# A three-part network on one core: its first stage written in the order of a list scheduler, the token-mixing remainder spread over three channel steps, and the causal mask moved to VectorE

## The chip, the cores and the metric

The kernel runs on one core of one Trainium2 chip, in one launch. The metric is device time in microseconds (us), median of several runs. Engines are named as in the profile: PE is TensorE (matmuls and transposes), PEld its weight loads, DVE is VectorE, ACT is ScalarE, POOL is GpSimd, SP is SyncE, which issues all transfers here.

## The reference, cut to what matters

Three layers follow each other (4 batches, 576 positions, width 512):

```
# 1: attention, 8 heads of width 64; 4x pooled attention plus a band of |i - j| < 4
out_d = sm_attn(mean4(q), mean4(k), mean4(v));  out_up = repeat(out_d, 4)
scores = where(|i - j| < 4, 0.125 * q k^T, -1e9);  out_local = softmax(scores) v
x = out_up + out_local
# 2: mixing over tokens (576 -> 256 -> 576), then over channels (512 -> 1536 -> 512)
u = x + (relu(x^T w_tok1) w_tok2)^T
x = u + relu(u w_ch1) w_ch2
# 3: four experts, each a causal attention head; the two best experts of a position count
scores = where(causal, -1e9, 0.125 * q k^T);  out += mask * weight * (softmax(scores) v wo)
```

The four mixing weights come in as float64 and are turned into a high and a low float32 part on the chip; a product of two such pairs is three matmuls.

## The kernel before, in words

**First stage.** The attention has 16 units (a batch `b` and a pair of heads `p`). A unit loads q, k and v (`load_qk`, `load_v`), computes local and pooled scores (`scores`: PE tiles `sl` and `sd`, row maxima on DVE in `nmx` and `nd`, exponentials on ACT, normalisation on POOL), transposes the weights (`turns`: `pdt`, `tl`) and multiplies with v (`values`: `pod`, `ol`; DVE adds into `u`). Two units make a half (8 halves), which goes through token mixing: transposes (`tx`, `tok_turn`), the first product (`h`, `tok_first`) and the second (`pu`, `tok_second`, added to `u` by DVE). Besides, 7 pieces of token weights and 6 pieces of channel weights are converted from float64 in this stage: per piece two ACT instructions (`t`, `g`), three of DVE (`a`, `f`, `f` again: L200 to L202), one add on POOL (L206), then the high part on ACT and the low part on DVE (L143, L153).

The loop at L508 calls these as whole steps, in the order given by `ORDER`, with priorities from `PRI`; the tile framework's own scheduler then lays out each engine's queue. All token weights are converted ahead of the loop (`START`, `tok_weights`), one channel piece per unit from the fourth on (`CONV0`).

**Channel stage.** `ch_step` (L569): 4 groups of hidden channels by 5 blocks of columns, 1440 matmuls of some 460 columns into tiles `c`. Token mixing of the last half is called ahead of the first steps (`TAIL`), which the scheduler fills in between.

**Third stage.** `score` (L712) computes one tile of scores of one expert: two matmuls `s<-K,Q`, and a third, `s<-caus,identb`, which adds -1e9 above the diagonal (80 tiles, one mask matmul each). DVE takes the row maximum (`nm`, L734), ACT the exponential from PSUM with the sum (L737), DVE the normalisation (L738 to L740). Projections, transposes (`pt`), products with v (`o`) and the output (`wo`) fill PE around them.

Every PE instruction but a transpose has line L108 in the profile, so tiles tell them apart.

Of the kernel before, what the change touches and what calls it, by code (L numbers as in the profile page):

```python
# [45 lines left out]
PRI = {'K': 100, 'a': 30, 'W': -60, 'S': 30}  # L46
VEC = {'k': 3, 'v': 1}
KTWICE = True
ZENG = ['any', 'any']
PRE = False  # L50
QPOOL = 'vector'
KPOOL = 'gpsimd'
ABANKS, CBANKS = (4, 2), (6, 1)
START = 'q0 q1 q2 v0 w v1 v2'
XLO = 'gpsimd'
CONV0 = 3
UB = 5
TAIL = [0, 3, 4, 3]
ULO = 'vector'
LA = 2  # L60
DELAY = 0
ORDER = 'VKTCFWS'
VB = 3
KB = 3


@with_exitstack
def body(ctx, tc, qT, kT, vw, vp, wt1, wt2, wc1, wc2, wq, wk, wvg, wo, out):
# [24 lines left out]
    def spare(kind, i=0):  # L93

        return nc.vector if i < VEC.get(kind, 0) else nc.gpsimd

# [20 lines left out]
    caus = cst.tile([128, TQ], BF16, name="caus")  # L117
# [7 lines left out]
    for hf in range(2):  # L125
# [6 lines left out]
    nc.gpsimd.affine_select(out=caus, in_=caus, compare_op=OP.is_ge, fill=-1.0e9, base=0,  # L132
                            pattern=[[-1, TQ]], channel_multiplier=1)
# [7 lines left out]

    def split(hi, lo, src, relu=False, scale=None):
        nc.scalar.activation(hi, src, AF.Relu if relu else AF.Copy, **({"scale": scale} if scale else {}))  # L143
        lowpart(lo, src, hi, relu, scale)
# [18 lines left out]
    def flat(t, shape):  # L163
        return t.rearrange("p c n -> p (c n)") if len(shape) == 3 else t

# [8 lines left out]
    def load_f32(dram, shape, name, dst=None):  # L174

        P0, n = shape[0], 1
        for d in shape[1:]:
            n *= d
        if dram.dtype == F32:
            if dst is None:  # L180
                dst = pv.tile(shape, F32, tag="w64t", bufs=2, name=name + "_t")
            nc.sync.dma_start(dst, dram)
            return dst
        raw = pv.tile([P0, n, 2], I32, tag="raw64", bufs=2, name=name + "_raw")
        d32 = dram.bitcast(I32)
        if len(shape) == 3:
            nc.sync.dma_start(raw.rearrange("p (c n) t -> p c (n t)", c=shape[1]), d32)
        else:
            nc.sync.dma_start(raw.rearrange("p n t -> p (n t)"), d32)
        h = raw[:, :, 1]  # L190
        a = pv.tile([P0, n], I32, tag="w64a", bufs=2, name=name + "_a")
        f = pv.tile([P0, n], I32, tag="w64f", bufs=2, name=name + "_f")
        g = pv.tile([P0, n], F32, tag="w64g", bufs=2, name=name + "_g")
        t = pv.tile([P0, n], F32, tag="w64t", bufs=2, name=name + "_t")

        nc.scalar.activation(t.bitcast(I32), raw.bitcast(U32)[:, :, 0], AF.Copy, scale=2.0 ** -29)  # L196

        nc.scalar.activation(g, h.bitcast(F32), AF.Abs)

        nc.vector.tensor_scalar(a, h, 3, 0x3FFFFFF8, op0=OP.logical_shift_left, op1=OP.bitwise_and)  # L200
        nc.vector.scalar_tensor_tensor(f, h, -0x40000000, a, op0=OP.bitwise_and, op1=OP.bitwise_or)
        nc.vector.scalar_tensor_tensor(f.bitcast(F32), g, 2.0 ** -15, f.bitcast(F32), op0=OP.is_ge, op1=OP.mult)  # L202
        if dst is None:
            dst = t.rearrange("p (c n) -> p c n", c=shape[1]) if len(shape) == 3 else t

        nc.gpsimd.tensor_tensor(flat(dst, shape).bitcast(I32), f, t.bitcast(I32), op=OP.add)  # L206
        return dst
# [20 lines left out]
    def tok_split(dram, shape, name):  # L228
        hi = pt.tile(shape, F32R, name=name + "_hi")
        lo = pt.tile(shape, F32R, name=name + "_lo")  # L230
        split(flat(hi, shape), flat(lo, shape), flat(load_f32(dram, shape, name), shape))
        return hi, lo

    tok = {}

    def tok_weights():
        w1 = []
        for t in range(0, 4, 2):
            hi, lo = tok_split(wt1[128 * t:128 * t + 256].rearrange("(t p) j -> p t j", t=2), [128, 2, DT], f"wt1_{t}")
            w1 += [(hi[:, i], lo[:, i]) for i in range(2)]  # L240
        wr = [pt.tile([128, DT], F32R, name=f"wt1_r{x}") for x in "hl"]
        nc.gpsimd.memset(wr[1][REM:].bitcast(F32), 0.0)
        src = load_f32(wt1[512:S], [REM, DT], "wt1_4")
        split(wr[0][:REM], wr[1][:REM], src)
        nc.scalar.activation(wr[0][REM:], src, AF.Copy)
        tok["w1"] = w1, wr
        w2 = [[tok_split(wt2[m * 128:(m + 1) * 128, s * HS:(s + 1) * HS], [128, HS], f"wt2_{m}{s}")
               for s in range(2)] for m in range(2)]
        tok["w2"] = w2


# [8 lines left out]
    Vl, Vd = {}, {}  # L260

    def load_v(b, p):
        i = b * NP + p
        if i < VB:
            zero(VZ, i, getattr(nc, ZENG[1]))
            nc.gpsimd.memset(VX[i], 0.0)
        Vl[b, p] = VZ[(b * NP + p) % VB]
        for h in range(2):
            nc.sync.dma_start(Vl[b, p][64 * h:64 * h + 64, h], vw[b, p, 64 * h:64 * h + 64])
        raw = pa.tile([112, 3, 4, D], F32, tag="vp", bufs=1, name=f"vp{b}{p}")  # L270
        nc.sync.dma_start(raw, vp[b, p])
        vd = pa.tile([112, 2, D], F32, tag="vd", bufs=3, name=f"vd{b}{p}")
        vx = VX[(b * NP + p) % VB]
        i = b * NP + p
        spare("v", i).tensor_tensor(raw[:, :, 0:2], raw[:, :, 0:2], raw[:, :, 2:4], op=OP.add)
        spare("w", i).tensor_tensor(vd, raw[:, 0::2, 0], raw[:, 0::2, 1], op=OP.add)
        nc.gpsimd.tensor_tensor(vx[:64, 0], raw[:64, 1, 0], raw[:64, 1, 1], op=OP.add)
        nc.gpsimd.tensor_tensor(vx[64:112, 1], raw[64:, 1, 0], raw[64:, 1, 1], op=OP.add)
        Vd[b, p] = (vd, vx)

    QK = {}

    def load_qk(b, p):
        q = pa.tile([128, S], F32, tag="qT", bufs=3, name=f"qT{b}_{p}")
        nc.sync.dma_start(q, qT[b, p])
        i = b * NP + p
        if i < KB:
            zero(KZ, i, getattr(nc, ZENG[0]))
        kz = KZ[i % KB]
        for h in range(2):  # L290
            nc.sync.dma_start(kz[64 * h:64 * h + 64, h], kT[b, p, 64 * h:64 * h + 64])
        k = None
        if KTWICE:
            k = pa.tile([128, S], F32, tag="kT", bufs=3, name=f"kT{b}_{p}")
            nc.sync.dma_start(k, kT[b, p])
        QK[b, p] = (q, k, kz)

    SC = {}

    def scores(b, p):  # L300
        qt, kt, kz = QK.pop((b, p))

        def pool4(d, x, eng):
            x4 = x.rearrange("p (g r) -> p g r", r=4)
            if eng == "vector":
                nc.vector.tensor_reduce(d, x4, axis=AX.X, op=OP.add)
            else:
                a = pa.tile([128, SD, 2], F32, tag="pool2", bufs=2, name="pool2")[:d.shape[0]]
                nc.gpsimd.tensor_tensor(a, x4[:, :, 0:2], x4[:, :, 2:4], op=OP.add)
                nc.gpsimd.tensor_tensor(d, a[:, :, 0], a[:, :, 1], op=OP.add)  # L310

        qd = pa.tile([128, SD], F32, tag="qd", bufs=3, name="qd")
        kd = pa.tile([128, SD], F32, tag="kd", bufs=3, name="kd")
        pool4(qd, qt, QPOOL)
        if KTWICE:
            pool4(kd, kt, KPOOL)
        else:
            for h in range(2):
                o = slice(64 * h, 64 * h + 64)
                nc.vector.tensor_reduce(kd[o], kz[o, h].rearrange("p (g r) -> p g r", r=4), axis=AX.X, op=OP.add)  # L320

        ps = b2("sl")
        for h in range(2):
            mm(ps[:, h, :NW * 32].rearrange("p (t k) -> p t k", k=WIN), identb,
                             band[:, None, :].to_broadcast([128, NW // 2, WIN]), start=True, stop=False)
        for w in range(NW):
            o, g = 64 * (w % 2), 2 * (w // 2)
            cols = slice(KS[w], KS[w] + WIN)

            for h0, h1 in [(0, 2)] if g != NT - 1 else [(0, 1), (1, 2)]:  # L330
                bk, c0 = (g + h0) // NT, (g + h0) % NT * WIN
                mm(ps[o:o + 64, bk, c0:c0 + (h1 - h0) * WIN].rearrange("p (h k) -> p h k", k=WIN),
                                 qt[:, cols], kz[:, h0:h1, cols], start=False, stop=(g + h1) % NT == 0)
        sv = ps[:, :, :NW * 32].rearrange("p b (t k) -> p b t k", k=WIN)
        nmx = pa.tile([128, 2, NT], F32, tag="nmx", bufs=3, name="nmx")
        nc.vector.tensor_reduce(nmx, sv, axis=AX.X, op=OP.max, negate=True)
        nc.vector.tensor_scalar_mul(nmx, nmx, 0.125)  # L337
# [129 lines left out]
    for what in START.split():  # L467
        if what == "w":
            with ahead("I"):
                tok_weights()  # L470
# [464 lines left out]
```

## Time and profile before

| | |
|---|---|
| median of 3 runs | 740.4 us (740.32 to 742.41) |
| the profiled execution, its own time | 743.14 us |
| its span, first to last instruction | 741.4 us |
| PE busy in the span | 680.7 us, 92% |
| PEld | 593.2 us, 80% |
| DVE | 478.1 us, 64% |
| ACT | 387.5 us, 52% |
| POOL | 162.5 us, 22% |
| mean granted TensorE clock (1 is 2.4 GHz, 0.5 is 1.2 GHz) | 0.961 |

Busy time counts any instruction that has begun and not ended, also while it is held up inside; a matmul's end is modelled, and matmuls overlap, so a price of PE work is read from one start to the next. Shares over the whole span mix three stages: the first channel matmul starts at 219.0 us and the last ends at 529.1 us. "Idle before" is the time an engine waited ahead of an instruction, with what ended the wait.

### The profile page before, as it was taken

The numbers are of one execution on the slowest core, as the hardware profiler recorded it, in microseconds if no ns is written. First come the engines' busy times: TensorE is split into PE (matmuls) and PEld (weight loads), VectorE is DVE, ScalarE is ACT, GpSimd is POOL, SyncE is SP. The second block draws the span as 40 slices with busy tenths as digits, with TensorE's granted clock in tenths as the row PEclk, the third lists the DMA queues.
The fourth block names the chain that finished last, engine by engine and source line by source line (L and its number), as shares of the span: only waits on it lengthen the run. The fifth ranks groups of instructions, "written<-read, shape, count | busy, mean of one in ns | idle before, by whom it ended". The sixth has DMA issues, their size and how long they took to land.

```text
span 741.4 us, 13335 instructions
## 1 busy us (share of the span) xinstructions
PE 680.7 (92%) x4892; PEld 593.2 (80%) x4892; DVE 478.1 (64%) x1076; ACT 387.5 (52%) x1236; POOL 162.5 (22%) x197
## 2 busy tenths in 40 slices
PE   3468889889999999999999999999998999999987
PEld 2346777667888998888888898888886988889875
DVE  4899986556554796764665464443268777777873
ACT  6577667556643564433532232222157776686674
POOL 4777864443210222100110000000312030010000
PEclk8767899999999999999999999999999999999999
DMA  9978564423000231200101010000020022021102
GB/s 249 268 228 229 166 187 121 126 75 101 20 1 1 67 104 61 78 33 1 58 15 42 1 31 26 2 1 0 1 65 17 17 61 62 21 85 33 33 29 100
DMA packets 31761, 52.26 MB, mean 70 GB/s; under 512 B 3728, under 2 KB 16528, under 8 KB 31696
## 3 DMA queue, kind: packets, MB, share of 16 engines
q1 hardware_dynamic: 31696, 51.40, 23.8%
q8 instruction: 39, 0.64, 0.4%
q14 instruction: 26, 0.21, 0.1%
HBM read 41.95 MB, written 4.72 MB: 63 GB/s over the span
## 4 chain that ended last, share of the span: by engine, by line
PE 81%; DVE 8%; ACT 4%; DMA 3%; POOL 1%; issue 1%; SPq 0%; ACTq 0%; POOLq 0%; DVEq 0%
PE c L108 41%; PE proj L108 7%; PE vp L108 4%; PE s L108 4%; PE o L108 4%; PE h L108 3%; PE wo L108 3%; PE ol L108 3%; PE pu L108 3%; PE sl L108 3%; PE pt L111 3%; DMA qT<-in_qT_dram 2%; PE pod L108 2%; PE tx L111 1%; ACT P L343 1%
## 5 line engine op out<-in xcount | busy, mean ns | idle before, releaser
L108 PE MATMUL c<-hh,wcl 128*128 128x460 f32 (+1 forms) x240 | 89.2, 372 | 0.0
L108 PE MATMUL c<-uh,wcl 128*128 128x460 f32 (+1 forms) x240 | 89.2, 372 | 0.0
L108 PE MATMUL c<-ul,wch 128*128 128x460 f32 (+1 forms) x240 | 89.1, 371 | 0.0
L108 PE MATMUL c<-hl,wch 128*128 128x460 f32 (+1 forms) x240 | 89.1, 371 | 0.0
L108 PE MATMUL c<-hh,wch 128*128 128x460 f32 (+1 forms) x240 | 89.1, 371 | 0.0
L108 PE MATMUL c<-uh,wch 128*128 128x460 f32 (+1 forms) x240 | 89.1, 372 | 0.0
L143 ACT ACTIVATE hh<-c 128x460 fp32r<-128x460 f32 (+1 forms) x60 | 33.1, 551 | 98.9 <-PE c L108 98.4
L149 DVE SCALAR_TENSOR_TENSOR hl<-c,hh 128x460 fp32r<-128x460 f32 (+1 forms) x60 | 38.1, 634 | 53.4 <-ACT hh L143 53.3
L206 POOL TENSOR_TENSOR wc_t<-wc_f,wc_t 128x512 int32<-128x512 int32 x24 | 33.5, 1400 | 159.4 <-ACT wc_t L196 142.1
L541 ACT ACTIVATE uh<-u 128x460 fp32r<-128x460 f32 (+1 forms) x80 | 46.2, 586 | 34.6 <-PE c L108 23.5
L343 ACT ACTIVATE P<-sl,nmx 128x64 f32<-128x64 f32 x160 | 48.1, 332 | 26.4 <-DVE nmx L337 19.9
L542 DVE TENSOR_TENSOR ul<-u,uh 128x460 fp32r<-128x460 f32 (+1 forms) x80 | 49.8, 634 | 11.5 <-ACT uh L541 11.5
L737 ACT ACTIVATE Pc<-s,nm 112x576 f32<-112x576 f32 (+4 forms) x80 | 44.4, 560 | 16.0 <-DVE nm L734 15.8
L108 PEld LDWEIGHTS c<-hl,wch 128*128 128x128 f32 x240 | 45.2, 188 | 5.2
L108 PEld LDWEIGHTS c<-uh,wcl 128*128 128x128 f32 x240 | 45.2, 188 | 5.3
L108 PEld LDWEIGHTS c<-ul,wch 128*128 128x128 f32 x240 | 45.2, 188 | 5.1
L108 PEld LDWEIGHTS c<-uh,wch 128*128 128x128 f32 x240 | 45.1, 188 | 5.0
L108 PEld LDWEIGHTS c<-hh,wch 128*128 128x128 f32 x240 | 45.1, 188 | 5.1
L108 PEld LDWEIGHTS c<-hh,wcl 128*128 128x128 f32 x240 | 45.1, 188 | 5.0
L734 DVE TENSOR_REDUCE nm<-s 112x1 f32<-112x576 f32 (+4 forms) x80 | 40.5, 514 | 11.7 <-PE s L108 10.2
L108 PE MATMUL s<-K,Q 128*112 128x288 f32 (+3 forms) x192 | 42.7, 320 | 3.5 <-DVE Q L151 1.8
L740 DVE TENSOR_SCALAR Pc<-Pc,su,gw 112x576 f32<-112x576 f32 (+4 forms) x80 | 38.3, 480 | 2.3
(180 smaller groups left out, 1767.3 us busy)
## 6 DMA issues: line engine op xcount, KB each, us to landing
wc_raw<-in_wc_dram SPq DMA_DIRECT2D x24, 512.0 KB, 3.7
vp<-in_vp_dram SPq DMA_DIRECT2D x16, 336.0 KB, 3.4
vz<-in_vw_dram SPq DMA_DIRECT2D x32, 160.0 KB, 3.6
qT<-in_qT_dram SPq DMA_DIRECT2D x16, 288.0 KB, 4.3
kz<-in_kT_dram SPq DMA_DIRECT2D x32, 144.0 KB, 4.6
kT<-in_kT_dram SPq DMA_DIRECT2D x16, 288.0 KB, 4.5
K<-K SPq DMA_DIRECT2D x64, 72.0 KB, 2.0
out_dram<-y SPq DMA_DIRECT2D x18, 256.0 KB, 2.0
```

The costliest lines, as they stand in the source:

```text
L108: behind(nc.tensor.matmul(*a, **kw))
L111: behind(nc.tensor.transpose(*a))
L143: nc.scalar.activation(hi, src, AF.Relu if relu else AF.Copy, **({"scale": scale} if scale else {}))
L149: nc.vector.scalar_tensor_tensor(lo, src, 0.0, h, op0=OP.max, op1=OP.subtract)
L206: nc.gpsimd.tensor_tensor(flat(dst, shape).bitcast(I32), f, t.bitcast(I32), op=OP.add)
L343: nc.scalar.activation(P[:, t, h], sv[:, bk, i], AF.Exp, bias=nmx[:, bk, i:i + 1], scale=0.125, accum_out=sm[:, t, h:h + 1])
L541: nc.scalar.activation(hi, u, AF.Copy)
L542: getattr(nc, ULO).tensor_tensor(lo, u, hi.bitcast(F32), op=OP.subtract)
L734: nc.vector.tensor_reduce(nm[:nq], sv, axis=AX.X if t < 4 else AX.XY, op=OP.max, negate=True)
L737: nc.scalar.activation(pv_, sv, AF.Exp, bias=nm[:nq], accum_out=su[:nq])
L740: nc.vector.tensor_scalar(P[:nq, :n], P[:nq, :n], su[:nq], ST[b]["W"][:nq, t, 2 * p + e:2 * p + e + 1], op0=OP.mult, op1=OP.mult)
```

## The change

The first stage is now made of 25 kinds of single steps (`unit`, `half`, `convert_f64`; for example `sl`, `mx`, `ex`, `rs`, `P` in place of the first part of `scores`). `first_stage` writes down for each step its engine, a duration (`COST`), what it waits for, what buffers it holds, and a rank; `arrange` runs a list scheduler over them while the kernel is built, and the steps are issued in that order under a manual schedule, so each engine's queue has it. Conversions get ranks of their own (`CONV`): a token piece every 1.1 units from the start, a channel piece every 1.8 units from the fourth.

```diff
+CONV = (2.8, 11.1, 37.6, 17.7)
+SLACK = 0.17
...
+        op("mx", i, "DVE", [("sl", i, None)])
+        op("ex", i, "ACT", [("mx", i, None)], [("P", [("tl", i, 1)])])
...
+        t, r, n = min(can)
+        eng = ops[n][0]
+        t, r, n = min((c for c in can if ops[c[2]][0] == eng and c[0] <= t + SLACK), key=lambda c: (c[1], c[0]))
...
+    steps = arrange(first_stage())
+    cut = max(k for k, n in enumerate(steps) if n[0] in U_[0] or n[0] not in H_[0]) + 1
+    with tc.manual_schedule():
+        for n in steps[:cut]:
+            do(*n)
...
-    tail = [lambda i=i, w=w: tok_step(i, w) for i in range(n, n + 2 + DELAY) for w in "KFW"]
+    tail = steps[cut:]
+    share = -(-len(tail) // TAIL)
     for i in range(len(seq) + 1):
...
+        if i < TAIL:
+            with ahead("T"):
+                for n in tail[i * share:(i + 1) * share]:
+                    do(*n)
```

What is left of token mixing after the last attention step and conversion (`tail`) is split evenly over the first three channel steps. Three smaller edits in the first stage: the pooled product with `vx` is two matmuls of 64 output rows in place of one of 128; the first unit's v sum goes from DVE to POOL (`VEC` is gone); and the zeroing of buffers, which was shared out over DVE and ACT, is on DVE (k) and POOL (v).

```diff
-        mm(po[:, :SD], vx.rearrange("p h d -> p (h d)"), PdT[:, 1], start=False, stop=True)
+            for h in range(2):
+                mm(po[64 * h:64 * h + 64, :SD], vx[:, h], PdT[:, 1], start=False, stop=True)
```

In the third stage the mask matmul is gone. One DVE instruction adds a float32 mask to the scores, writes them negated to SBUF and takes their minimum; ACT reads them there. The mask constant grows from 116 columns of bf16 to 580 of float32.

```diff
-    caus = cst.tile([128, TQ], BF16, name="caus")
+    caus = cst.tile([128, NT * TQ], F32, name="caus")
...
-            if m0 < m1:
-                mm(ps[:nq, m0 - a0:m1 - a0], identb[:nq, :nq], caus[:nq, m0 - d0:m1 - d0],
-                                 start=False, stop=True)
...
-        nc.vector.tensor_reduce(nm[:nq], sv, axis=AX.X if t < 4 else AX.XY, op=OP.max, negate=True)
...
-        nc.scalar.activation(pv_, sv, AF.Exp, bias=nm[:nq], accum_out=su[:nq])
+        mask = caus[:nq, 4 * TQ - d0:4 * TQ + nq]
...
+        nc.vector.tensor_tensor_reduce(pv_, sv, mask, -1.0, 3.0e38, OP.add, OP.min, nm[:nq])
+        nc.scalar.activation(P[:nq, :n], P[:nq, :n], AF.Exp, bias=nm[:nq], scale=-1.0, accum_out=su[:nq])
```

How the queues moved, at three places. DVE in the first stage, before, where the third unit's maximum is taken; `wt_01`, `wt_10`, `wt_11` and `wc_0` are weight pieces, all else is of units:

```order
L337 TENSOR_SCALAR nmx<-nmx 128x10
L200 TENSOR_SCALAR wt_01_a<-wt_01_raw 128x288
L201 SCALAR_TENSOR_TENSOR wt_01_f<-wt_01_raw,wt_01_a 128x288
L202 SCALAR_TENSOR_TENSOR wt_01_f<-wt_01_g,wt_01_f 128x288
L357 TENSOR_REDUCE nd<-sd 72x4
L306 TENSOR_REDUCE qd<-qT_1_682 128x144
L200 TENSOR_SCALAR wt_10_a<-wt_10_raw 128x288
L358 TENSOR_SCALAR nd<-nd 72x4
L414 TENSOR_TENSOR u<-ol,OdT 128x232
L201 SCALAR_TENSOR_TENSOR wt_10_f<-wt_10_raw,wt_10_a 128x288
```

The same queue now, from the maximum of the fourth unit; the next conversion, that of `wt_01`, comes 31 rows behind the first of these:

```order
L462 TENSOR_REDUCE nmx<-sl 128x10
L463 TENSOR_SCALAR nmx<-nmx 128x10
L476 TENSOR_SCALAR rs<-sm 128x10
L477 RECIPROCAL rs<-rs 128x10
L565 TENSOR_TENSOR u<-ol,OdT 128x232
L565 TENSOR_TENSOR u<-ol,OdT 128x344
L492 TENSOR_REDUCE nd<-sd 72x4
L493 TENSOR_SCALAR nd<-nd 72x4
L428 TENSOR_REDUCE qd<-qT_1_518 128x144
```

Conversions stood between the steps of a unit and now stand units apart; all 7 token pieces had come ahead of the fifth unit's maximum and now reach to the eighth's.

PE at the end of the first stage, now, where the transposes of the seventh half (`tx`) and its first product (`h`) meet the first channel tile (`c`):

```order
L222 MATMUL pu<-wt_11h,h1l 128x288
L225 MATMUL tx_2880<-ident,u 128x128 x4
L225 MATMUL tx_2886<-ident,u 128x128 x4
L225 MATMUL tx_2894<-ident,u 64x128 x2
L222 MATMUL h_2905<-xh,wt_0h 128x256
L222 MATMUL h_2905<-xl,wt_0h 128x256
L222 MATMUL h_2905<-xh,wt_0l 128x256
L222 MATMUL h_2905<-xh,wt_0h 128x256
L222 MATMUL h_2905<-xl,wt_0h 128x256
L222 MATMUL h_2905<-xh,wt_0l 128x256
L222 MATMUL h_2905<-xh,wt_2h 128x256
L222 MATMUL c_2936<-uh,wch_114 128x462
```

Before, all of the seventh half stood ahead of the first `c`; now most of its first product, its second product and the whole eighth half follow behind it.

DVE in the third stage, now (a tile of 232, one of 576 columns); the fused instruction is followed by a second one that writes the minimum:

```order
L875 ISA Pc,nm<-s,caus 116x232
L875 ISA nm 116x1
L875 ISA Pc,nm<-s,caus 112x576
L875 ISA nm 112x1
L878 RECIPROCAL su<-su 116x1
```

Before, one TENSOR_REDUCE (L734) stood in the place of each such pair; there are 80 pairs.

## Rows read from the trace of the kernel before

**Rows 1.** Busy time by stretch: engine us (instructions), granted clock, DMA share, GB/s.
```profile
0.00:20.00 20.00, 7.53 (x68) 5.41 (x68) 10.04 (x20) 11.45 (x38) 9.16 (x29) 0.83 0.92 249
20.00:100.00 80.00, 57.60 (x551) 44.85 (x551) 74.65 (x125) 54.97 (x218) 61.27 (x70) 0.74 0.79 223
100.00:219.20 119.20, 110.31 (x1272) 92.39 (x1273) 70.51 (x162) 72.53 (x359) 45.89 (x63) 0.97 0.30 84
219.20:250.00 30.80, 30.66 (x171) 27.93 (x170) 16.46 (x31) 10.32 (x20) 0.00 (x0) 1.00 0.00 1
250.00:529.20 279.20, 279.11 (x1332) 250.18 (x1330) 161.72 (x266) 99.50 (x176) 23.11 (x18) 1.00 0.11 35
529.20:741.40 212.20, 195.46 (x1500) 172.49 (x1500) 144.69 (x478) 138.76 (x426) 23.11 (x18) 0.99 0.15 46
```
**Rows 2.** The chain that ended last, 20 to 260 us: start, us, what.
```profile
35.73 3.76 DVE nmx L337
...
210.26 3.36 PE h L108 x28
213.62 0.84 PE pod L108 x6
214.46 1.31 PE ol L108 x40
215.76 3.40 PE pu L108 x24
```
**Rows 3.** The same chain, its longest piece.
```profile
249.96 279.17 PE c L108 x1332
```
**Rows 4.** DVE groups from 20 to 100 us: busy, mean ns, idle before.
```profile
L202 DVE SCALAR_TENSOR_TENSOR wc_f<-wc_g,wc_f 128x512 f32<-128x512 f32 x8 | 8.7, 1096 | 0.0
L337 DVE TENSOR_SCALAR nmx<-nmx 128x10 f32<-128x10 f32 x6 | 7.9, 1322 | 0.0
L201 DVE SCALAR_TENSOR_TENSOR wc_f<-wc_raw,wc_a 128x512 int32<-128x512 int32 x8 | 7.6, 955 | 0.0
L200 DVE TENSOR_SCALAR wc_a<-wc_raw 128x512 int32<-128x512 int32 x8 | 5.9, 741 | 1.7 <-DMA wc_raw<-in_wc_dram 1.7
...
L153 DVE TENSOR_TENSOR wcl<-wc_t,wch 128x512 fp32r<-128x512 f32 x6 | 4.8, 796 | 0.0
```
**Rows 5.** DVE instructions of three lines over the run: ns min/median/max.
```profile
L337 DVE TENSOR_SCALAR nmx<-nmx x16: 156/172/3818, 11.8 to 200.1; 128x10 f32<-128x10 f32 x16
L202 DVE SCALAR_TENSOR_TENSOR wc_f<-wc_g,wc_f x24: 630/684/1980, 53.8 to 373.1; 128x512 f32<-128x512 f32 x24
L200 DVE TENSOR_SCALAR wc_a<-wc_raw x24: 409/418/2189, 51.3 to 369.5; 128x512 int32<-128x512 int32 x24
```
**Rows 6.** PE in order of time, 117 to 132 us: start, us, instructions.
```profile
117.39 0.45 PE L108 MATMUL sl<-band,identb 128*128 128x320 bf16 x2
...
129.03 1.28 PE L108 MATMUL sl<-kz,qT 128*64 128x128 f32 x23
130.24 0.72 PE L108 MATMUL sd<-kd,qd 64*72 64x144 f32 x8
130.90 0.59 PE L111 MATMUL pdt<-ident,Pd 72*112 72x72 f32 x6
131.32 0.71 PE L111 MATMUL tl<-ident,P 128*128 128x128 f32 x5
```
**Rows 7.** PE in order of time in the third stage.
```profile
584.36 0.40 PE L108 MATMUL s<-K,Q 128*116 128x256 f32 x2
584.59 0.21 PE L108 MATMUL s<-caus,identb 116*116 116x116 bf16 x1
584.65 0.56 PE L111 MATMUL pt<-ident,Pc 116*116 116x116 f32 x4
```
**Rows 8.** DVE groups of the third stage, 529.2 to 741.4 us.
```profile
L739 DVE RECIPROCAL su<-su 116x1 f32<-116x1 f32 x64 | 10.3, 161 | 1.7
L734 DVE TENSOR_REDUCE nm<-s 116x1 f32<-116x464 f32 x16 | 10.1, 639 | 6.0 <-PE s L108 5.8
```
**Rows 9.** A DVE group of the channel stage: two inputs, one in PSUM, one in SBUF.
```profile
L565 DVE TENSOR_TENSOR acc<-c,acc 128x462 f32<-128x462 f32 x16 | 10.2, 637 | 7.5 <-PE c L108 7.0
```

More of the change, by code (lines that the diff above doesn't have):

```diff
@@ new lines, in arrange @@
+def arrange(ops):
+    end, order, todo = {}, [], dict(ops)
+    free = dict(PE=4.0, ACT=1.0, DVE=3.0, POOL=4.0, SP=0.6)
+    held = {k: [] for k in HELD}
+    wire, window, warm, busy = 0.0, 0, True, 0.0
+    while todo:
+        can = []
+        for n, (eng, cost, deps, hold, after, r) in todo.items():
+            waits = [q for tag, rd in hold if len(held[tag]) >= HELD[tag] for q in held[tag][-HELD[tag]]]
+            if any(d not in end for d in deps) or any(d in todo for d in after) or any(q not in end for q in waits):
+                continue
+            t = max([free[eng]] + [end[d] + (0.09 if ops[d][0] != eng else 0) for d in deps] + [end[q] + 0.09 for q in waits])
+            can.append((t, r, n))
+        t, r, n = min(can)
+        eng = ops[n][0]
+        t, r, n = min((c for c in can if ops[c[2]][0] == eng and c[0] <= t + SLACK), key=lambda c: (c[1], c[0]))
+        eng, cost, deps, hold, after, r = todo.pop(n)
+        order.append(n)
+        if eng == "SP":
+            for kb in cost:
+                t += 0.5
+                wire = max(wire, t + 1.0) + kb * 0.00366
+            free[eng], end[n] = t, wire + 0.9
+        else:
+            if eng == "PE":
+                while t >= (window + 1) * 3.413:
+                    warm = busy >= (0.66 if warm else 0.93) * 3.413
+                    window, busy = window + 1, 0.0
+                cost *= 1 if warm else 2
+                busy += cost
+            free[eng] = end[n] = t + cost
+        for tag, rd in hold:
+            held[tag].append(rd)
+    return order
@@ L258, in zero @@
             eng.memset(tiles[i][64 * h:64 * h + 64, 1 - h], 0.0)
[L260 to L296, printed above, removed]
@@ L431, in tok_turn, with high @@
+        def high(g):
             if g == 2:
[L432 to L453 removed]
@@ L467, in body @@
[L467 to L470, printed above, removed]
-        else:
-            (load_qk if what[0] == "q" else load_v)(*units[int(what[1])])
-    n = len(units)
-    for u in units[:2]:
-        with ahead("S"):
-            scores(*u)
-    with ahead("T"):
-        turns(*units[0])
+                x = pt.tile([128, 256], F32R, tag="xr", bufs=1, name="xr")
+                r["x", g] = x, x[:REM], x[REM:], r["tx", g][:REM, 0]
+            else:
+                hi = pt.tile([128, 2, 256], F32R, tag=f"xh{g}", bufs=1, name="xh")
+                lo = pt.tile([128, 2, 256], F32R, tag=f"xl{g}", bufs=1, name="xl")
+                r["x", g] = (hi, lo), hi, lo, r["tx", g]
@@ L481, in wset, with add @@
+        def add(x):
+            j, s = divmod(x, 2)
+            u = U[b][:, 2 * hf + j, s * HS:(s + 1) * HS]
+            nc.vector.tensor_tensor(u, r["pu", x][:, :HS], u, op=OP.add)
+        return dict(tx=turn, xh=high, xl=low, h=first, hh=hidden_high, hl=hidden_low, pu=second, ua=add)
     def wset(p, tag):
```

584 lines of the change are left out of this document (339 added, 245 removed).

## Prediction

> **What bounds the kernel now.** I read the busy time by stretch first, since a mean over three stages says little. Behind 250 us PE is busy in 279.11 of 279.20 us [rows 1]: the channel stage is matmul after matmul, 1332 in 279.17 us, 0.2096 us each [rows 3], and nothing of this change makes them fewer. From 20 to 100 us it is another picture: DVE is busy for 74.65 of 80 us (93%), PE for 57.60, at a mean clock of 0.74 [rows 1], so part of that PE time ran at 1.2 GHz. From 100 to 219.2 us it turns round: PE 110.31 of 119.2 us (93%), DVE 70.51 (59%). So the first stage has two halves, one that waits for DVE and one that waits for PE.
>
> What DVE does in the first half says why. The four lines of channel weight conversion take 8.7 + 7.6 + 5.9 + 4.8 = 27.0 us of its 74.65 [rows 4], and the token pieces come on top, all ahead of the units that PE could work on. The other thing to see there is L337, a multiplication of ten numbers per partition: 0.172 us in the median, 3.8 at most [rows 5], and 3.76 us of one instance lie on the chain that ended last [rows 2]. POOL is busy for 61.27 of those 80 us [rows 1]; DVE instructions that read SBUF are held up while it works. L200 and L202 show the same (medians 418 and 684 ns against means of 741 and 1096) [rows 4, 5].
>
> How much could be had at most? Price the PE work of the stage at the 2.4 GHz level, from one start to the next. A unit: `sl` 0.45 + 1.26 (24 matmuls at the pace of 23 in 1.21), `sd` 0.66, `pdt` 0.42, `tl` 0.6 [rows 6], `pod` 0.84, `ol` 1.31 [rows 2], together 5.5; sixteen are 88. A half: 28 of `h` 3.4, 24 of `pu` 3.4 [rows 2], ten transposes at the pace of `tl` 1.4, together 8.2; eight are 66. So 154 us. The channel stage ends at 529.2; less its 1440 x 0.2096 = 302 us that leaves 227 us for 154 us of work: 73 us are lost to idle PE and to the lower clock, nearly all ahead of 219 us.
>
> **The change, part by part.** *The order of the first stage.* No work goes away; it is spread. Up to 20 us I change nothing: the first unit's chain (load, scores, maximum, exponential, sum, normalisation, transpose) is the same, and PE does two units' `sl` and `sd` there, 4.7 us of work. After that two engines share the bound. DVE: 10.04 + 74.65 + 70.51 = 155.2 us ahead of 219.2 [rows 1]. What moves behind the first `c` is the seventh half's `h` low part and four additions, about 2.5 us (an estimate, from two-input rows of the same kind, 0.64 us for 462 columns [rows 9]); the first unit's v sum, under 1 us, goes to POOL, which has room. That leaves 152, and 142 behind the first 20 us. If DVE is kept as busy as it was from 20 to 100 us, 93%, these take 152 us, and the first `c` starts at 172. PE has by then to do 154 - 4.7 - 14 = 135 us in the same 152, 89%; from 100 to 219.2 us it was busy for 93%, so that is feasible, and with fewer gaps I expect the clock near the 0.97 of that stretch instead of 0.74 [rows 1]. The 14 us are what now stands behind the first `c`: most of the seventh half's `h`, its `pu`, and the eighth half, 2.6 + 3.4 + 1.4 + 3.4 + 3.4. They delay the channel matmuls by their own time and no more, as the 8 us of them did before: from 219.2 to 250 us PE was busy for 30.66 of 30.80 [rows 1]. So 172 + 14 = 186 in place of 227: **-41 us**.
>
> *The small edits there.* Two `vx` products of 64 rows for one of 128: between nothing, if two of 64 share the time of one, and double the time, at most 0.45 us a unit (half of `pod` [rows 2]) or 7 us; I take nothing, because the two `vd` products of `pod` already have that form and the four together take 0.84. Zeroing and the longer mask constant lie on POOL and DVE in the first 20 us, in which POOL is busy for 9.16 [rows 1]: cover for a microsecond or two; without it, that much is added once. On the queue of SP the loads of the units now stand ahead of most conversions' loads; the transfers are busy for 0.79 of the time from 20 to 100 us, and 0.30 after [rows 1], so spreading them takes pressure off.
>
> *The mask.* 80 matmuls go; the slot of one is 584.65 - 584.59 = 0.06 us [rows 7], so 4.8 us of PE, in a stage in which PE is busy for 195.46 of 212.20 us [rows 1]: -4.5. DVE: the nearest row for the fused instruction is the addition with one input in PSUM, 637 ns for 462 columns [rows 9], against 639 for the maximum over 464 [rows 8]; I take the same price. A floor under it is nothing saved, since each element must still be read once; the ceiling is both passes in turn, 637 more for such a tile. Each now has a second instruction that writes the minimum, one number per partition: nothing to 0.161, the price of a reciprocal of one number [rows 8]; at 0.15 it is 12 us on a DVE that is busy for 144.69 of 212.20 [rows 1]. PE has other tiles' work meanwhile, except at the end, where tiles follow each other with nothing in between: some ten times 0.15, +1.5. ACT reads the same columns from SBUF. Its bank of PSUM comes free one step earlier, worth nothing while PE waits elsewhere. Sum of the part: **-3 us**.
>
> Against the profiled execution, 743.1 - 41 - 3 = 699. The median of the runs shown lies 2.7 us below that execution, so I predict **697 us**. (0.3%, 2 us, is about what can be told from no change.)
>
> **Rivals.** *A: the waits on POOL grow.* Now DVE and POOL are both dense for the whole stage, not for 80 us. Over the stage these waits are some 21 us (an estimate: means above medians, 1.15 x 6 for L337, 0.41 x 8 for L202, 0.32 x 8 for L200 [rows 4, 5], 12.7 us from 20 to 100 us, and the rest from the lines of the same kind). If they double, 142 + 21 at 93% is 175, the first `c` starts at 195, and the gain shrinks to 18: 743.1 - 18 - 3 - 2.7 = 719. For it: the steps' durations in the change are near the medians, so a late step is followed by others in a fixed order. Against it: POOL's work is the same, over a longer stretch than those 80 us. The Trainium skill (SBUF — State Buffer, "Who interferes with whom") says that VectorE and GpSimd share a pair of ports under an exclusive lock, and that the loser blocks for the other's whole instruction; by that rule this rival would be the outcome. Rows 4 and 5 agree that it happens, not that it must grow.
>
> *B: the order does better.* If DVE's waits shrink by half, it needs 131 at 93% = 141 us, and PE 135 at 95% = 142: first `c` at 162, gain 51, 687.
>
> *C: the fused instruction is dear.* It has no row. DVE has 67 us free in the third stage [rows 1]. If each of 80 cost 1.4 us more, 111 us, that room and all of the 44 us gained would be gone; at 2 us more the kernel would end at 743.1 - 41 - 4.5 + 160 - 67 - 2.7 = 788, slower. That is three passes or more over the tile; one more pass (the ceiling above) stays inside the room and costs little.
>
> *D: the fixed order stalls.* A step written too early holds its engine's queue, and all behind it: DVE's maximum behind a piece of weights that has not come, say. If PE loses its 73 us again, only the mask is left: 737, a gain at the edge of what can be told.
>
> **How the numbers follow.** Forecast 0.60, A 0.18, B 0.12, D 0.04, C 0.06. The forecast's own spread is DVE between 90 and 96% in the stage, -47 to -36, and the mask part between -4.5 and 0. The range goes from B's side, 682, to A's with the mask worth nothing, 722. That leaves out D, C and the far ends of A and B, under 2 in 10. Faster by over 0.3%: the forecast, A, B and half of D, whose 3 us are near that bound: 0.92. Within 0.3%: the other half of D, 0.02. Slower by over 0.3%: C, 0.06.
>
> **What would show it.** In the changed profile the first `c` starts at 165 to 180 us; DVE stays above 85% and PE above 80% in every 20 us from 30 us on; the clock is above 0.9 from 60 us; no conversion stands in a row with three others. L463 (the former L337) has a mean under 0.5 us; over 0.8 speaks for A. The channel matmuls still take 0.2096 us each. In the third stage the fused instruction takes 0.6 to 0.75 us at 464 columns and the stage is 209 us long, give or take 2. Wrong would be a first `c` after 200 us, or a third stage above 212.

## The result, and the profile after

The changed kernel takes 716.2 us in the median (714.9 to 723.3) against 740.9 us before: ratio 0.968, 95% interval [0.962, 0.975]. That is faster, by 24.7 us, inside the range of 682 to 722 and 19 us short of the 697 forecast. The profiled execution took 715.17 us, its span is 713.4 us (741.4 before).

Busy time by stretch of the changed kernel, with the columns of [rows 1]: stretch, length, PE, PEld, DVE, ACT and POOL us (instructions), granted clock, DMA share, GB/s.

```profile
0.00:20.00 20.00, 8.61 (x68) 6.15 (x68) 16.92 (x29) 11.05 (x43) 13.96 (x29) 0.86 0.94 263
20.00:40.00 20.00, 17.22 (x213) 13.50 (x213) 14.98 (x34) 15.53 (x85) 18.07 (x29) 0.72 0.78 204
40.00:60.00 20.00, 13.95 (x157) 11.05 (x157) 16.42 (x33) 16.95 (x91) 14.42 (x20) 0.91 0.87 225
60.00:80.00 20.00, 18.30 (x295) 15.67 (x294) 15.68 (x38) 15.74 (x81) 14.75 (x20) 1.00 0.78 216
80.00:100.00 20.00, 16.94 (x205) 14.88 (x206) 16.84 (x35) 16.93 (x80) 13.95 (x18) 0.91 1.04 249
100.00:120.00 20.00, 17.40 (x216) 15.36 (x211) 18.48 (x34) 14.96 (x65) 15.83 (x20) 0.91 0.61 179
120.00:140.00 20.00, 16.65 (x200) 14.69 (x200) 18.39 (x33) 13.00 (x44) 13.53 (x14) 1.00 0.70 193
140.00:160.00 20.00, 14.25 (x175) 11.24 (x174) 17.21 (x37) 13.56 (x64) 12.27 (x16) 1.00 0.26 79
160.00:180.00 20.00, 19.38 (x270) 17.99 (x269) 9.94 (x23) 11.27 (x57) 5.68 (x7) 1.00 0.12 36
180.00:200.00 20.00, 18.85 (x159) 17.43 (x158) 11.77 (x22) 8.72 (x18) 0.00 (x0) 1.00 0.00 1
```

The picture of before, DVE full in one half and PE full in the other, is gone. From 20 to 160 us DVE is busy for 75 to 92% of each 20 us, PE for 70 to 92%, ACT for 65 to 85%, so none of the three is full any more. (GpSimd has one stretch at 90%, from 20 to 40 us, and the transfers are dense up to 100 us: 0.78 to 1.04 of the time.) Then DVE falls to half, and PE finishes alone for 30 us.

The chain that ended last, from the last pieces of the first stage on (start, us, what):

```profile
189.72 2.52 PE c L222 x12
193.50 4.62 PE c L222 x22
198.12 1.68 PE h L222 x14
200.45 0.70 DVE h1l L266
201.20 2.64 PE pu L222 x18
203.84 15.17 PE c L222 x72
219.81 3.37 PE h L222 x28
223.91 3.43 PE pu L222 x24
227.34 279.14 PE c L222 x1332
```

The first channel matmul (`c`) starts at 189.6 us, before at 219. The last one starts at 506.1. Its end less the 302 us of all 1440, as in the prediction, gives a first stage of 204.3 us where it was 227 (this is what "first stage" means in the tables below): 22.7 of the 28 us between the two spans. The channel matmuls themselves are as before [rows 3]: 1332 in 279.14 us. The other 5 us are in the third stage, 207.1 us for 212.2; first its busy time, then two groups of the fused instruction and the small instruction behind it:

```profile
506.30:713.40 207.10, 191.04 (x1421) 168.58 (x1420) 144.73 (x558) 140.41 (x426) 23.23 (x18) 0.99 0.16 47
```

```profile
L875 DVE CUSTOM_DVE_ANT_0 Pc<-s,caus 116x464 f32<-116x464 f32 x16 | 10.3, 641 | 6.6 <-PE s L222 6.4
...
L875 DVE DVE_READ_ACCUMULATOR2_ANT nm<- 116x1 f32 x64 | 5.3, 83 | 0.0
```

PE's busy time fell from 195.46 [rows 1] to 191.04 us, by 4.4, and the fused instruction takes what the maximum took: 641 ns against 639 [rows 8].

### The profile page after: what moved, and what is told of

Read it like the earlier page. It is cut to its first block, busy times and chain, and to the rows that moved or that the text cites. A ratio compares the mean times of both kernels' runs of the same rounds, so it can differ in the third digit from the quotient of the medians.

```text
span 713.4 us, 13279 instructions
## 1 busy us (share of the span) xinstructions
PE 657.8 (92%) x4844; PEld 580.6 (81%) x4844; DVE 476.4 (67%) x1156; ACT 384.5 (54%) x1229; POOL 168.8 (24%) x204
## 4 chain that ended last, share of the span: by engine, by line
PE 75%; DVE 10%; ACT 8%; POOL 3%; DMA 3%; issue 2%; ACTq 0%; POOLq 0%; DVEq 0%
PE c L222 42%; PE proj L222 7%; PE vp L222 4%; PE o L222 4%; PE wo L222 3%; PE s L222 3%; ACT P L471 3%; PE pt L225 3%; PE h L222 2%; PE pu L222 2%; DMA vp<-in_vp_dram 1%; PE sl L222 1%; DMA qT<-in_qT_dram 1%; ACT PT L901 1%; PE ol L222 1%
## 5 line engine op out<-in xcount | busy, mean ns | idle before, releaser
L471 ACT ACTIVATE P<-sl,nmx 128x64 f32<-128x64 f32 x160 | 47.5, 338 | 10.8 <-DVE nmx L463 8.5
L876 ACT ACTIVATE Pc<-Pc,nm 112x576 f32<-112x576 f32 (+4 forms) x80 | 46.8, 588 | 10.0 <-DVE nm L875 9.8
L875 DVE CUSTOM_DVE_ANT_0 Pc<-s,caus 112x576 f32<-112x576 f32 (+4 forms) x80 | 40.8, 517 | 13.2 <-PE s L222 12.0
```

Source lines behind the costliest of these rows:

```text
L471: nc.scalar.activation(P[:, t, h], r["sl"][:, bk, j], AF.Exp, bias=r["nmx"][:, bk, j:j + 1], scale=0.125, accum_out=sm[:, t, h:h + 1])
L875: nc.vector.tensor_tensor_reduce(pv_, sv, mask, -1.0, 3.0e38, OP.add, OP.min, nm[:nq])
L876: nc.scalar.activation(P[:nq, :n], P[:nq, :n], AF.Exp, bias=nm[:nq], scale=-1.0, accum_out=su[:nq])
```

## The experiments

The theory: the new order spreads DVE's work as planned, but DVE can't be kept at 93% in it, because each engine now waits for another in turn. Rivals for the missing 19 us: DVE waits for GpSimd (rival A), loads that come late, a fixed order that stalls, or a mask part that took more than its share. Unless said otherwise, each kernel is the changed kernel with one edit. Times are medians, with the ratio to the kernel before on the same chip; the changed kernel's own is 0.968 [0.962, 0.975]. Times within the trace (first `c`, first stage) come from one execution each.

**The mask alone**, in the kernel before.

```diff
-    caus = cst.tile([128, TQ], BF16, name="caus")
+    caus = cst.tile([128, NT * TQ], F32, name="caus")
...
-                mm(ps[:nq, m0 - a0:m1 - a0], identb[:nq, :nq], caus[:nq, m0 - d0:m1 - d0],
-                                 start=False, stop=True)
...
+        nc.vector.tensor_tensor_reduce(pv_, sv, mask, -1.0, 3.0e38, OP.add, OP.min, nm[:nq])
```

Expected: 

> The kernel before with the mask edit alone (longer constant, fused add-and-minimum on VectorE, 80 mask matmuls gone); the first stage keeps its old order. By the prediction this part is worth -3 us: 738 against 741. By the changed kernel's trace, in which the third stage lasts 205.5 us where it was 211.6, it is worth -6: 735, and then the new order of the first stage earned only some 19 to 20 of the 41 us it was priced at. If the third stage owes its gain to the new first stage in some way (clock, timing of the last conversions), this run is at 738 to 741 and its third stage at 209 or more.

Measured: 735.8 us, ratio 0.992 [0.990, 0.995], that is -5.6 us (-3.9 to -7.5). Its third stage is 208.3 us long, 3.9 less than before. So by the time the mask part earned somewhat more than its forecast 3, and the order of the first stage about 19 of 41.

**The order not fixed**: the same steps, in the same order in the text, without the manual schedule.

```diff
-    with tc.manual_schedule():
-        for n in steps[:cut]:
-            do(*n)
+    for n in steps[:cut]:
+        do(*n)
```

Expected: 

> The changed kernel with the same single steps written in the list's order, but without the manual schedule: the framework's scheduler may reorder them by its own costs. If what the change earns comes from the single steps in that order of writing, this stays within 3 us of 716. If it comes from the order being fixed on each engine's queue, this is slower, up to 735 (the first stage's gain lost, the mask's kept). If the fixed order is what stalls (a step that waits holds those behind it, the prediction's rival D in small), this is faster, 700 to 710, with the first channel matmul before 180 us.

Measured: 740.1 us, ratio 0.998 [0.996, 1.000]. The first `c` comes at 212.7 us. Here the framework's scheduler lays out the queues again. Single steps alone earn nothing: the whole gain of the first stage, and some more (740.1 against 735.8 with the mask alone), is in the list's order being kept. Rival D, by which the kept order stalls until only the mask is left, falls as a cause for the whole.

**Two buffers for the pooled-value load.**

```diff
-            r["vp"] = pa.tile([112, 3, 4, D], F32, tag="vp", bufs=1, name=f"vp{b}{p}")
+            r["vp"] = pa.tile([112, 3, 4, D], F32, tag="vp", bufs=2, name=f"vp{b}{p}")
```

Expected: 

> The changed kernel with two buffers for the pooled-value load instead of one, the order of all steps unchanged. In the changed kernel this load waits on its queue for 23 us in all until GpSimd has read the buffer, 8.06 us of one such load lie on the chain that ended last, and loads of q behind it on the queue come late (6.57 us on the chain). If late loads cost the missing 19 us, the first channel matmul moves from 189.7 to 175 to 183 us and the time to 702 to 710. If the stage is held by the durations of the compute steps in their fixed order, loads that come earlier change nothing beyond 2 us: 714 to 718.

Measured: 719.9 us, ratio 0.970 [0.966, 0.973]: no difference that can be told. The waits on SP's queue in the first 190 us (us in all, times, longest), of the changed kernel and then of this one:

```profile
SPq L424 <- POOL vx L443: 23.0, 7, 6.0
SPq L422 <- PE ol L222: 17.6, 3, 8.2
SPq L409 <- PE sl L222: 13.6, 5, 5.9
```

```profile
SPq L409 <- PE sl L222: 21.1, 6, 9.3
SPq L422 <- PE ol L222: 17.1, 3, 8.2
```

The wait for GpSimd is gone from the head of the list; the waits for PE were there before, and one of them grew. The load of 8.06 us is off the chain, but the loads did not come earlier as a whole: from 20 to 190 us GpSimd waited for this load for 12.0 us where it had been 10.0 (L440), and other loads (5.4 to 7.7 us) lie on the chain instead. So this one wait on the queue is not the cause. Whether late loads are is not shown, because the edit did not bring them forward.

**Less work for DVE and GpSimd**, in four cuts: without the two scalings of the maxima; with the two normalisations on GpSimd cut to four columns; with the v sums cut to four columns; all three.

```diff
-            nc.vector.tensor_scalar_mul(nmx, nmx, 0.125)
...
-            nc.gpsimd.tensor_tensor(r["P"], r["P"], r["rs"][:, :, :, None].to_broadcast([128, NT, 2, WIN]), op=OP.mult)
+            nc.gpsimd.tensor_tensor(r["P"][:, :, :, :4], r["P"][:, :, :, :4], r["rs"][:, :, :, None].to_broadcast([128, NT, 2, 4]), op=OP.mult)
...
-            nc.gpsimd.tensor_tensor(raw[:, :, 0:2], raw[:, :, 0:2], raw[:, :, 2:4], op=OP.add)
+            nc.gpsimd.tensor_tensor(raw[:, :, 0:2, :4], raw[:, :, 0:2, :4], raw[:, :, 2:4, :4], op=OP.add)
```

Expected, no scaling: 

> The changed kernel without the two scalings of the maxima (a multiplication of ten and one of four numbers per partition for each of 16 units); the exponentials use unscaled maxima, the order of all other steps is unchanged. In the changed kernel these 32 instructions keep VectorE busy for 14.9 us, of which 32 x 0.17 = 5.4 us would be left without waiting. If VectorE's own work sets the stage's length (its 152 us ahead of the first channel matmul, spread over 190 us), the first channel matmul comes 13 to 18 us earlier and the time is 698 to 704. If the stage is held by the fixed order as a whole, in which each engine waits in turn for another, a part comes back: 705 to 712. If it is held by PE or by loads, 714 to 718. The exponential reaches its maximum one VectorE instruction earlier too, so a gain over 15 us speaks for the chain of one unit rather than for VectorE's load.

Expected, small normalisations: 

> The changed kernel with GpSimd's two normalisations of each unit cut down to a sixteenth and a thirty-sixth of their columns, the order unchanged; most of the weights in the two score tiles stay unnormalised. GpSimd loses about 16 x (1.26 + 1.16 - 0.5) = 31 us of its 122 us ahead of the first channel matmul, and the chain from the sum to the transposes loses about 2 us in each unit. If VectorE's waits beside a working GpSimd are what the missing 19 us went to, this gains 8 to 14 us, and the cut in the v sums (the next run) gains as much; if it is the unit's chain through GpSimd, this gains 8 us or more and that one nothing; if neither, both stay at 714 to 718.

Expected, small v sums: 

> The changed kernel with GpSimd's four additions that form the pooled v of each unit cut down to a sixteenth of their columns, the order unchanged; most of the pooled v is left as zero. GpSimd loses about 16 x (2.55 - 1.0) = 25 us. These sums are not behind the scores, so the unit's chain of scores, exponential and transposes stays as long as it was. If VectorE's waits beside a working GpSimd cost the missing 19 us, the mean of the short scaling of ten maxima falls from 0.50 us to under 0.35 and the time is 704 to 710; if not, 713 to 718, with that mean unchanged or with the wait moved elsewhere.

Expected, all three: 

> The three cuts of the last runs together (no scaling of the maxima, both normalisations and the v sums of GpSimd cut to a few columns), order unchanged; the output is not the reference's. Alone they gave 4, 7 and 2 us. If the loss is made of waits and latencies that add, this is 702 to 705 and the first channel matmul at 176 to 180; if one of them uncovers the next, less: 706 to 709; if the order runs as its own short prices say once VectorE no longer waits for GpSimd, the first channel matmul is at 168 to 174 and the time 696 to 701.

Measured:

| cut | median us | ratio | first `c` | first stage |
|---|---|---|---|---|
| no scaling | 712.4 | 0.961 [0.958, 0.964] | 185.0 | 199.8 |
| normalisations | 709.3 | 0.953 [0.950, 0.957] | 183.9 | 198.6 |
| v sums | 714.4 | 0.962 [0.959, 0.964] | 184.4 | 199.1 |
| all three | 706.2 | 0.950 [0.946, 0.955] | 178.8 | 193.5 |

By the time, only the second and the last are clear of the changed kernel's interval: the normalisations brought 7 us, the v sums nothing that can be told apart. By the first stage the three single cuts are alike, 4.5 to 5.7 us shorter than 204.3. With the v sums cut, GpSimd had 21 us less to do (122.45 to 101.34) and the scaling of ten maxima (L465 there) fell from 496 ns in the mean to 294; what sets that run apart is a third stage of 211.8 us, which the edit does not touch. So these runs do not tell GpSimd's load from the unit's own chain. The last line matters most. From 20 us to the first `c`, the changed kernel and then the one with all three cuts:

```profile
20.00:189.60 169.60, 142.52 (x1810) 122.19 (x1811) 135.25 (x275) 122.56 (x566) 108.50 (x140) 0.94 0.61 163
```

```profile
20.00:178.80 158.80, 140.56 (x1804) 123.22 (x1802) 112.66 (x244) 121.13 (x562) 57.52 (x136) 0.92 0.69 175
```

DVE has 22.6 us less to do, GpSimd 51.0, and the first `c` comes 10.8 us earlier. DVE's share falls from 80 to 71%. The stage doesn't follow DVE's work one for one.

**True prices.** The list is made by a table of prices (for 40 kinds of steps in all), and the trace shows longer steps. DVE groups of the changed kernel up to 190 us:

```profile
L462 DVE TENSOR_REDUCE nmx<-sl 128x10 f32<-128x640 f32 x16 | 12.9, 806 | 1.8 <-PE sl L222 1.8
L492 DVE TENSOR_REDUCE nd<-sd 72x4 f32<-72x576 f32 x16 | 11.9, 742 | 3.8 <-PE sd L222 3.8
...
L463 DVE TENSOR_SCALAR nmx<-nmx 128x10 f32<-128x10 f32 x16 | 7.9, 496 | 0.6
...
L330 DVE TENSOR_SCALAR wc_a<-wc_raw 128x512 int32<-128x512 int32 x10 | 7.4, 753 | 0.0
L337 DVE SCALAR_TENSOR_TENSOR wc_f<-wc_g,wc_f 128x512 f32<-128x512 f32 x10 | 7.1, 715 | 0.7 <-ACT wc_g L326 0.2
L493 DVE TENSOR_SCALAR nd<-nd 72x4 f32<-72x4 f32 x16 | 7.0, 437 | 0.5
...
L270 DVE TENSOR_TENSOR wcl<-wc_t,wch 128x512 fp32r<-128x512 f32 x6 | 6.1, 1012 | 0.1
```

`mx` is priced at 1.0 us and takes 0.806 + 0.496 = 1.30; `md` 0.95, takes 1.18; `a` 0.43, takes 0.75; `lo` 0.68, takes 1.01. Times their counts that is 16 x 0.30 + 16 x 0.23 + 10 x 0.32 + 6 x 0.33 = 13.7 us of DVE that the order doesn't know of. Three kernels are to tell prices from ranks: true prices (those measured in the changed kernel) with ranks (and the two constants beside them, `CONV` and `SLACK`) searched anew for them; the old prices with ranks searched for as long; true prices with the old ranks.

```diff
-    lq=0.55, qd=0.76, kd=1.45, pv=2.1, sl=1.85, mx=1.0, ex=2.95, rs=0.42, P=1.26, sd=0.65, md=0.95, ed=1.42,
+    lq=0.55, qd=0.74, kd=1.35, pv=2.6, sl=1.8, mx=1.33, ex=3.0, rs=0.48, P=1.28, sd=0.66, md=1.22, ed=1.57,
...
-    q=-25.9, v=-9.3, qd=-32.3, kd=45.9, pv=5.7, sl=2.5, mx=-0.7, ex=-25.2, rs=-61.0, P=-3.5, sd=-14.1, md=24.9,
+    q=-24.2, v=-14.1, qd=-79.6, kd=-29.7, pv=0.3, sl=80.2, mx=-43.8, ex=-20.3, rs=-23.5, P=-41.0, sd=-23.2, md=17.9,
```

Expected, true prices and new ranks: 

> The changed kernel with the list's price table replaced by the durations that the changed kernel's trace shows (maximum with its scaling 1.33 for 1.0, maximum of the pooled scores 1.22 for 0.95, first shift of a conversion 0.76 for 0.43, its low part 1.02 for 0.68, v sums 2.6 for 2.1, and so on) and with its ranks set anew for these prices; same steps, same instructions, another order. If the missing 19 us are the price of an order made for shorter steps (each step late, and those behind it in the fixed queues too), the first channel matmul comes at 172 to 178 us and the time is 694 to 704. If the order is not what holds the stage, but the sum of the work and the waits of whatever order, it stays at 712 to 718.

Expected, old prices and new ranks: 

> The changed kernel with its own price table, and ranks set anew by the same search, as long, as the ranks of the re-planned kernel: by the old prices its order is 10 us shorter than the changed kernel's. If the re-planned kernel's gain (704 for 716) came from the true durations in the table, this one, made for the old ones, gains a part at most: 709 to 716. If it came from more search and the prices do not matter, this is at 702 to 707 as well.

Expected, true prices and old ranks: 

> The changed kernel with the measured durations in the price table and its old ranks, which were set for the old prices. If true prices alone make the order better, this is 700 to 712. If a list by ranks is good only for the prices that the ranks were set for, this is slower than the changed kernel although each price is nearer to the chip: 722 to 732, the first channel matmul after 200 us.

Measured:

| prices, ranks | median us | ratio | first `c` | first stage |
|---|---|---|---|---|
| true, new | 704.1 | 0.948 [0.944, 0.951] | 185.3 | 194.1 |
| old, new | 716.1 | 0.965 [0.962, 0.968] | 194.7 | 203.5 |
| true, old | 731.0 | 0.985 [0.982, 0.987] | 203.5 | 218.2 |

With the same steps and instructions, 12 us of the missing 19 came back, and the kernel beats both others. (Its first `c` is later than expected, because 17 more steps of the end of token mixing stand ahead of it; its first stage is 10.2 us shorter than the changed kernel's.) More search at the old prices gave nothing, which speaks for the prices; true prices with ranks made for other ones are worse than both. Each table was searched once, so how much of the 12 us is the luck of a search is not shown.

How far the chip runs behind its list can be read as well. `arrange`, run by itself, gives the time at which the list ends each step by its own prices. Take the last attention step, `ad` of the sixteenth unit (L565): in the changed kernel its last instruction starts at 182.8 us and ends at 183.3.

```profile
L565 DVE TENSOR_TENSOR u<-ol,OdT x32: 347/490/649, 31.1 to 182.8; 128x232 f32<-128x232 f32 x16, 128x344 f32<-128x344 f32 x16
```

| kernel | its end by the list, us | in the trace, us |
|---|---|---|
| changed (old prices and ranks) | 164.1 | 183.3 |
| true, new | 170.0 | 180.0 |
| old, new | 164.8 | 189.4 |
| true, old | 198.3 | 197.2 |

At the old prices the chip is 19 and 25 us late, at the true ones 10 late and 1 early. In the changed kernel the lag grows from 2 us at the first unit to 19 at the last. The third kernel's poor time stands in its list already.

The same stretch of the first kernel of the first table:

```profile
20.00:185.30 165.30, 146.73 (x1871) 128.77 (x1871) 133.15 (x282) 126.09 (x575) 105.37 (x136) 0.94 0.61 166
```

DVE is at 81%, as before the edit (80%); PE went from 84 to 89%: it idles for 18.6 us of this stretch instead of 27.1.

**A second turn**: prices from the trace of that kernel, 0.5 us more for a load, and ranks (with `CONV` and `SLACK`) for the mean over six disturbed tables. The edit to the price of a load:

```diff
-            free[eng], end[n] = t, wire + 0.9
+            free[eng], end[n] = t, wire + 1.4
```

Expected: 

> A second turn of the re-planned kernel: prices from its own trace (first shift 0.65, merge 0.87, scaled product 0.88, low part 0.75, half a microsecond more for a load to land), ranks chosen for the mean over six tables in which single steps are longer or shorter at random. If the stall of the re-planned kernel at 155 to 175 us (conversions that wait for their load hold VectorE's queue) was what kept it from its plan, this is 696 to 702. If what is left is PE's own work and clock, 702 to 706.

Measured: 710.0 us, ratio 0.956 [0.953, 0.959], first stage 200.8 us: a miss, 6 us slower than the first turn. Its last attention step is due at 169.4 us by the list and ends at 184.7. So prices taken from a trace of the order, and a new search for them, can also lose; as three things changed at once, the runs do not say which did it. The chain of the first turn, and then that of this one, around the end of the list:

```profile
158.88 1.45 DVE wc_a L330 x2
160.33 0.61 DVE wc_f L333
160.99 4.54 DMA wc_raw<-in_wc_dram
...
169.54 0.60 DVE wc_f L333
170.14 0.61 DVE h1l L266
170.80 2.08 PE pu L222 x12
```

```profile
164.91 4.77 DMA wc_raw<-in_wc_dram
169.70 1.29 DVE wc_a L330
171.00 0.61 DVE h1l L266
...
178.78 5.01 DMA wc_raw<-in_wc_dram
```

This is rival D in small: a conversion whose load is late holds DVE's queue, and `hl` behind it keeps PE from `pu`. The first turn has it once, the second twice. That these stalls make the difference is not shown; an order that loads these weights earlier wasn't tried.

**The end of token mixing in one piece**, ahead of the first channel step.

```diff
-TAIL = 3
+TAIL = 1
```

Expected: 

> The changed kernel with the end of token mixing (what is left of the sixth half, the seventh and the eighth) written ahead of the first channel step and not in thirds ahead of the first three. By the prediction the end of token mixing delays the channel matmuls by its own time and no more, wherever it stands: then nothing changes beyond what PE idles inside this end, 716 to 720. If the thirds are what fills PE's waits between 190 and 227 us, this is slower by more than 4 us: 721 to 726, with the dense channel matmuls from 231 us on or later.

Measured: 719.2 us, ratio 0.965 [0.960, 0.969]: no difference that can be told. In its profile the first stage is 209.2 us long, 4.9 more, but the last attention step is 3.4 us late already, ahead of the edited part. The thirds among the channel steps earn nothing that shows.

## Why the prediction was right, and where it was off

*What bounds.* Right. There were two halves with different limits, and mixing them gained: with the mask's 5.6 us taken off, 19 us are left of the 24.7. The Trainium skill (Perfetto Trace Analysis, "Optimization Strategy") says that regimes with different most-contended engines may gain by being interleaved; the trace agrees (DVE 93% and then PE 93% before [rows 1], neither after), and the run without the fixed order adds that interleaving in the text alone gave nothing.

*DVE's work.* Priced at 152 us up to the first `c`, measured 152.17: right by luck in part. Counted by the groups of both traces, only some 0.4 us of work went away on balance (two additions and one `h` low part moved behind, the v sum left, but two `ul` of the channel stage and more zeroing came ahead); the other 2.4 us are instructions that took less time. That DVE would do only 10 of them in the first 20 us was wrong: it did 16.92.

*The step that failed* is "if DVE is kept as busy as it was from 20 to 100 us, 93%". From 20 us to the first `c` it was busy for 135.25 of 169.6 us, 80%, and the first `c` came at 189.6 instead of 172. The 93% had been read in a stretch with a stock of conversions ready to run (at most 1.7 us of idle time ahead of a group [rows 4]); spreading that stock is what the change does, so the likely reading, which no run isolates, is that the figure went with it. Two runs show that DVE's share was the wrong thing to divide by at all: with 22.6 us less DVE work (and 51 less on GpSimd) the first `c` came 10.8 us earlier, where 22.6 at 93% would be 24, and the re-planned kernel gained 12 us with DVE at 81%. The list could have told: from 20 us to its last attention step it plans DVE for some 78% and PE for 87%, at its own short prices. Its plan agrees with the forecast all the same, since 164.1 and the 6.3 us that lie between this step and the first `c` in the trace make 170.4, against 172. The Trainium skill (Perfetto Trace Analysis, "Identifying the Most-Contended Engine") has the engine of highest occupancy optimised first, with TensorE judged by its weight loads. By that it is DVE here (80%; ACT and the weight loads 72% each); with the scalings cut DVE had 9.3 us less to do from 20 us on, and the first `c` came 4.6 us earlier: it helps, by half of the cut.

*What took its place.* A fixed order that the chip runs behind, by 19 us at the last attention step. The table's prices leave out 13.7 us of DVE's time, nearly all of it in scalings, shifts and low parts, which read SBUF beside a GpSimd that is busy for 64% of the stretch, and a late step holds what stands behind it in its queue. Re-planned at true prices the kernel gave 12 us back, though a second turn kept only 6 of them. The other 7 are not settled: GpSimd's work (each of its cuts shortened the first stage by 5 to 6 us, but in an order with the old prices), loads and conversions that come late in DVE's queue, and PE partly at 1.2 GHz between 20 and 40 us (granted clock 0.72) are seen, none was isolated in the re-planned kernel.

*PE's check*, 135 us in 152 at 89%: the share was possible (89% in the re-planned kernel), but the changed kernel reached 84%, at a clock of 0.94.

*The 14 us behind the first `c`*: 204.3 - 189.6 = 14.7. Right, and the run with the end in one piece agrees as far as can be told.

*The small edits*, costed at nothing: right for the two `vx` products. Eight `pod` matmuls take 0.64 to 0.71 us in the chain, six took 0.84 [rows 2]. Not for the zeroing that went to GpSimd: two pieces (L399, 0.58 and 0.67 us) lie on the chain at 20 us.

*The mask*, -3: right in kind, small by the time of the run with it alone (-5.6). PE gave 4.4 of the 4.5; the second instruction takes 0.083 us, inside its bounds of nothing to 0.161; the 1.5 us at the end did not show. The third stage is 207.1 us long here, just inside the 207 to 211 given, and 208.8 in the median over the 13 kernels with the fused instruction that were profiled (207.1 to 211.8), 3.4 less than before.

*Rival A* came out near in time (719) and wrong in kind. The 716.2 lies inside the range only because the range was drawn out to A's price; as A's mechanism did not come, that is luck. By the excess over the medians of [rows 5], the waits of its three lines over the first stage did not double but shrank. Before (mean 663, 1032, 676 ns) and after:

```profile
L337 DVE TENSOR_SCALAR nmx<-nmx 128x10 f32<-128x10 f32 x16 | 10.6, 663 | 0.2
L202 DVE SCALAR_TENSOR_TENSOR wc_f<-wc_g,wc_f 128x512 f32<-128x512 f32 x10 | 10.2, 1032 | 0.0
...
L200 DVE TENSOR_SCALAR wc_a<-wc_raw 128x512 int32<-128x512 int32 x10 | 6.7, 676 | 1.7 <-DMA wc_raw<-in_wc_dram 1.7
```

That is 16 x 0.49 + 10 x 0.35 + 10 x 0.26 = 14 us before, and 16 x 0.32 + 10 x 0.03 + 10 x 0.34 = 9 us after, by the rows of the price table above. L463's mean of 0.496 us is just under the 0.5 named. Other lines waited longer (L493, 437 ns in the mean for 313; L270 on channel weights, 1012 for 796), so over all of DVE it is the 2.4 us of above. A little less waiting, and still late; that true prices in the table gave 12 us back says that the waits count where the order doesn't allow for them. *Rival B* (waits halved, 687) had the right sign for the waits and the wrong time, since it too divided DVE's work by 93%. *C* fell at the first look at the fused instruction; *D* lives on as the stall at the end of the list.

Of the other signs named, the clock was above 0.9 from 60 us on in the stretches shown, as said; DVE above 85% and PE above 80% in every 20 us was not met (DVE 78%, PE 70% at the lowest from 40 to 160 us).

## What to carry to other kernels

When two regimes are mixed, don't divide one engine's work by the share it had while the other engines' work was out of its way; if a list makes the order, read the shares that it plans. A fixed order can be no better than its prices: compare the list's times with a trace, step by step, and where the chip lags, put measured prices in, waits included, and search the order again for them, since new prices with old ranks were worse here than either. Measure each new order: the same turn gave 12 us once and lost 6 the next time. A load at the head of a chain is a cause only if bringing it forward moves the end, and a second buffer alone need not bring it forward.

## What the runs showed of the hardware

A ten-number multiplication on DVE can wait for two GpSimd instructions in a row. The changed kernel, in order of time (start, us, engine, line):

```profile
146.57 1.01 POOL L440 TENSOR_TENSOR vp<-vp 112x384 f32<-112x384 f32 x1
146.64 2.28 DVE L463 TENSOR_SCALAR nmx<-nmx 128x10 f32<-128x10 f32 x1
147.54 1.28 POOL L340 TENSOR_TENSOR wc_t<-wc_f,wc_t 128x512 int32<-128x512 int32 x1
```

It began 0.07 us behind the first, and ended 0.1 us behind the second. The Trainium skill (SBUF — State Buffer, "Who interferes with whom") says that the loser of the shared ports blocks for the other's whole instruction; here it lasted over two. Not every instruction that reads SBUF is held up, as the prediction has it: the sums of q on DVE (`qd`, L306, from SBUF) took 734 to 754 ns in all 16 instances of the kernel before. With GpSimd's normalisations cut, the longest instance of this line was 0.672 us:

```profile
L463 DVE TENSOR_SCALAR nmx<-nmx x16: 172/174/672, 11.8 to 157.0; 128x10 f32<-128x10 f32 x16
```

The fused add-and-minimum reads PSUM, adds a mask from SBUF, writes SBUF and reduces in the time of the plain maximum, 641 against 639 ns for 464 columns, plus 83 ns for the number that it leaves.
